# Eight batches one by one, or four pairs of batches as nine full row tiles with a written engine order

## The chip, the cores and the metric

The kernel runs on one core of one Trainium2 chip. The metric is the device time of one execution in microseconds (us): the median of several runs. Beside the runs stands one profiled execution, with the times of every instruction and DMA packet. TensorE (PE) multiplies matrices into PSUM, VectorE (DVE) and ScalarE (ACT) do element-wise work and empty PSUM, GpSimd (POOL) issues the weights' DMAs, and SyncE (SP) issues the other DMAs.

## The reference, cut to what matters

Linear attention with elu+1 as its feature map, for 8 batches, 8 heads, 576 rows and 64 columns a head, and then a mixer block on the heads put side by side (512 columns): token mixing over the 576 rows, channel mixing over the 512 columns.

```python
def phi(x):                                    # q, k, v: (8, 8, 576, 64), f32
    return np.where(x > 0, x, np.exp(x) - 1.0) + 1.0
q_p, k_p = phi(q), phi(k)
kv  = np.einsum('bhsd,bhse->bhde', k_p, v)
z   = np.sum(k_p, axis=2)
num = np.einsum('bhsd,bhde->bhse', q_p, kv)
den = np.einsum('bhsd,bhd->bhs', q_p, z)[..., None] + 1e-06
x = (num / den).transpose(0, 2, 1, 3).reshape(8, 576, 512)
h = np.maximum(x.transpose(0, 2, 1) @ w_tok1, 0.0) @ w_tok2      # 576x256, 256x576
u = x + h.transpose(0, 2, 1)
out = u + np.maximum(u @ w_ch1, 0.0) @ w_ch2                     # 512x1536, 1536x512
```

## The kernel before

One batch is 576 rows: four row tiles of 128 and one of 64, which takes as many instructions as a full one. Matmul operands are bf16, sums f32 in PSUM.

For each batch `emit_load` (L87) issues 15 DMAs on SP: q, k and v, each by row tile. A partition holds one row of the sequence; for each head 64 floats lie together in memory, so the packets are of 256 bytes. Two buffers of each are there. The weights are cast to bf16 by DMAs of POOL at the start (L58 to L73).

`emit_phi_v` (L113) makes phi on ScalarE and VectorE: exp to bf16 (L103), min with 1 (L106), then max(x, 0) plus that (L108); v is cast (L118, L120) with a column of ones behind each head, so that the product with k gives z too. `emit_kv` (L149) multiplies k and v for two heads at a time over five row tiles into one PSUM tile, which ScalarE copies into a block-diagonal `kv_sb` (L165, L167). `emit_qt` (L128) transposes q on TensorE, 20 transposes a batch, and ScalarE copies them. `emit_num_stile` (L171) gives numerator and denominator of one row tile in four matmuls into `nd_ps` (two PSUM buffers, shared with the k-v product and q's transposes under the tag "attn"); VectorE takes the reciprocal (L181) and multiplies (L182) into `x_sb`.

`emit_mm1` and `emit_mm2` are the token mixing: 10 matmuls of 512 columns, relu on ScalarE (L208), 10 more, the sum u on VectorE (L228), 20 transposes of u (L235) and their copies to `uT` (L245). `emit_mm3` (L253) is the first channel product: two halves of 288 rows, for each 12 blocks of 128 channels, 4 matmuls of 288 columns into `c_ps` (two PSUM buffers), relu on ScalarE to `cr` (L267). `emit_mm4` (L271) is the second: for each of the five row tiles 12 matmuls of 512 columns into `h2_ps` (called h_ps in the profile, L278), the sum on VectorE (L283), and the store (L285).

The last loop takes the batches in turn; attention of the next batch is written between the two channel products and, one numerator tile for each row tile, inside the second one. The order on each engine is then the scheduler's, which moves ready work forward: in the trace transposes of the next batch stand among the first channel product's matmuls.

## Time and profile before

| | us |
|---|---|
| median of 3 runs (382.64 to 384.41) | 384.29 |
| span of the profiled execution, first to last instruction | 382.6 |
| TensorE busy in it | 315.2 |
| ScalarE, VectorE busy | 168.7, 162.6 |
| first channel matmul of batch 0 starts at | 63.97 |
| one late batch, first channel product to the next one's (272.7 to 311.7) | 39.0 |

The time of the profiled execution outside its span is not shown. The page gives engines' busy time, but a matmul's time there holds its latency, so in a row of matmuls what counts is the time of the row divided by their number. Waiting is read from the idle time in brackets before an instruction, with the instruction that ended it.

### The profile page before, as it was taken

To read this page: it belongs to the slowest core of one execution; us is meant where nothing else is said; L and a number is where in the kernel's file an instruction comes from. 1 tells how busy PE (TensorE), PEld (TensorE's weight loads), DVE (VectorE), ACT (ScalarE), POOL (GpSimd) and SP (SyncE) were. 2 spreads that over 40 slices of the span, in tenths; PEclk is the share of its full clock that TensorE was granted. 3 is DMA by queue.
4 is the path that set the end of the run, shared out by engine and by line. 5 is a ranking of instruction groups with operands and counts; after the bars stand their busy time and mean duration, and the time that the engine had idled before them with its cause. 6 is when DMAs were issued, how large, how long until landed. Compare 5 with 4: busy or idle time off the path is not lost.

```text
span 382.6 us, 5083 instructions
## 1 busy us (share of the span) xinstructions
PE 315.2 (82%) x2022; PEld 178.7 (47%) x2048; DVE 162.6 (42%) x272; ACT 168.7 (44%) x297; POOL 13.0 (3%) x29
## 2 busy tenths in 40 slices
PE   0020756999879998999899988999999989978995
PEld 0020413665546545655465445645664556433642
DVE  1034467059576466456592349034402350232012
ACT  0304342780576436860884078504660366013620
POOL 7330000000000000000000000000000000000000
PEclk9999975999969999999999999999999999995999
DMA  9999999305997379637991760021002100210012
GB/s 178 205 205 207 215 214 210 70 3 158 195 207 116 77 198 212 131 84 192 203 215 32 199 139 0 2 87 38 0 2 83 43 1 2 82 41 2 0 55 71
DMA packets 121032, 41.82 MB, mean 109 GB/s; under 512 B 113520, under 2 KB 115888, under 8 KB 121008
## 3 DMA queue, kind: packets, MB, share of 16 engines
q1 hardware_dynamic: 117760, 37.76, 47.2%
q0 software_dynamic: 3248, 3.74, 5.6%
q8 instruction: 16, 0.26, 0.3%
q14 instruction: 8, 0.07, 0.1%
HBM read 35.78 MB, written 9.44 MB: 118 GB/s over the span
## 4 chain that ended last, share of the span: by engine, by line
PE 67%; SPq 11%; ACT 9%; DVE 6%; DMA 4%; issue 3%; DVEq 0%; ACTq 0%
PE c_ps L261 28%; PE h_ps L278 26%; SPq L94 11%; PE a_ps L204 4%; ACT uT L245 3%; DMA k_raw<-in_k_dram 3%; PE ut_ps L235 2%; PE kv_ps L155 2%; ACT qT L145 2%; PE h_ps L224 2%; DVE u_sb L228 2%; DVE q_p_e L108 1%; PE nd_ps L175 1%; ACT k_p_e L103 1%; ACT q_p_e L103 1%
## 5 line engine op out<-in xcount | busy, mean ns | idle before, releaser
L261 PE MATMUL c_ps<-uT,w_ch_sb 128*128 128x288 bf16 x768 | 113.3, 289 | 2.7 <-ACT uT L245 0.8
L278 PE MATMUL h_ps<-w_ch_sb,cr 128*128 128x512 bf16 (+1 forms) x467 | 105.0, 380 | 0.6
L261 PEld LDWEIGHTS <-w_ch_sb 128*128 128x128 bf16 x768 | 74.7, 98 | 38.9 <-issue 20.2
L267 ACT ACTIVATE cr<-c_ps 128x288 bf16<-128x288 f32 x192 | 77.8, 410 | 29.9 <-PE c_ps L261 23.4
L283 DVE TENSOR_TENSOR o_sb<-h_ps,u_sb 128x512 f32<-128x512 f32 (+1 forms) x40 | 27.5, 688 | 120.2 <-PE h_ps L278 116.9
L278 PEld LDWEIGHTS <-cr 128*128 128x128 bf16 (+1 forms) x480 | 47.2, 100 | 52.9 <-issue 2.1
L208 ACT ACTIVATE ar<-a_ps 128x512 bf16<-128x512 f32 x16 | 8.9, 595 | 92.0 <-PE a_ps L204 92.0
L228 DVE TENSOR_TENSOR u_sb<-h_ps,x_sb 128x512 bf16<-128x512 f32 (+1 forms) x40 | 27.5, 688 | 40.5 <-PE h_ps L224 40.5
L138 PE MATMUL qt_ps<-identity,q_p_e 128*128 128x128 bf16 x160 | 13.0, 231 | 24.2 <-POOL identity masks.py:199 24.2
L245 ACT COPY uT<-ut_ps 128x1024 bf16<-128x1024 bf16 (+1 forms) x24 | 20.9, 870 | 25.8 <-PE ut_ps L235 25.8
L235 PE MATMUL ut_ps<-identity,u_sb 128*128 128x128 bf16 x160 | 18.1, 245 | 15.5 <-DVE u_sb L228 15.3
L224 PE MATMUL h_ps<-ar,w_tok_sb 128*128 128x512 bf16 (+1 forms) x74 | 28.1, 442 | 1.7 <-ACT ar L208 1.0
L155 PE MATMUL kv_ps<-v_sb,k_p_e 128*128 128x130 bf16 (+1 forms) x160 | 18.9, 233 | 12.0 <-DVE v_sb L118 12.0
L103 ACT ACTIVATE k_p_e<-k_raw 128x2048 bf16<-128x2048 f32 (+1 forms) x16 | 20.0, 1267 | 19.7 <-DMA k_raw<-in_k_dram 14.4
L182 DVE TENSOR_TENSOR x_sb<-nd_ps,rden 128x512 bf16<-128x512 f32 (+1 forms) x40 | 26.9, 678 | 0.6
L235 PEld LDWEIGHTS <-u_sb 128*128 128x128 bf16 x160 | 10.8, 106 | 28.2 <-DVE u_sb L228 27.8
L108 DVE SCALAR_TENSOR_TENSOR q_p_e<-q_raw,q_p_e 128x2048 bf16<-128x2048 f32 (+1 forms) x16 | 23.6, 1482 | 0.2
L108 DVE SCALAR_TENSOR_TENSOR k_p_e<-k_raw,k_p_e 128x2048 bf16<-128x2048 f32 (+1 forms) x16 | 23.4, 1478 | 0.1
L138 PEld LDWEIGHTS <-q_p_e 128*128 128x128 bf16 x160 | 10.8, 104 | 26.4 <-DVE q_p_e L108 21.6
L175 PE MATMUL nd_ps<-kv_sb,qT 128*128 128x130 bf16 (+1 forms) x160 | 17.9, 242 | 6.1 <-ACT qT L145 2.8
L103 ACT ACTIVATE q_p_e<-q_raw 128x2048 bf16<-128x2048 f32 (+1 forms) x16 | 20.1, 1267 | 6.0 <-DMA q_raw<-in_q_dram 6.0
L155 PEld LDWEIGHTS <-k_p_e 128*128 128x128 bf16 (+1 forms) x160 | 12.2, 100 | 21.1 <-DVE v_sb L118 12.3
(27 smaller groups left out, 129.9 us busy)
## 6 DMA issues: line engine op xcount, KB each, us to landing
q_raw<-in_q_dram SPq DMA_DIRECT2D x32, 256.0 KB, 5.0
k_raw<-in_k_dram SPq DMA_DIRECT2D x32, 256.0 KB, 5.2
v_raw<-in_v_dram SPq DMA_DIRECT2D x32, 256.0 KB, 4.6
out_dram<-o_sb SPq DMA_DIRECT2D x32, 256.0 KB, 2.1
w_ch_sb<-in_moe_w_ch_dram POOLq DMA_DIRECT2D x4, 384.0 KB, 9.7
w_ch_sb<-in_moe_w_ch_dram POOLq DMA_DIRECT2D x12, 128.0 KB, 8.3
q_raw<-in_q_dram SPq DMA_DIRECT2D x8, 128.0 KB, 4.7
...
```

Of the source, the lines that this page charges most:

```text
L94: nc.sync.dma_start(out=tl[:sz, i, :, :], in_=src)
L103: nc.scalar.activation(out=e[:p, lo:hi], in_=flat_in[:p, lo:hi], func=AF.Exp)
L108: nc.vector.scalar_tensor_tensor(out=e[:p, lo:hi], in0=flat_in[:p, lo:hi], scalar=0.0, in1=e[:p, lo:hi], op0=ALU.max, op1=ALU.add)
L155: nc.tensor.matmul(out=kv_ps[:, j // 2, j % 2, 0:2 * (D + 1)], lhsT=k_p[:sz, i, 2 * j:2 * j + 2, :], rhs=v_sb[:sz, i, 2 * j:2 * j + 2, :], ...
L224: nc.tensor.matmul(out=h_ps[:sz], lhsT=w_tok2_sb[:, kt, 128 * ms:128 * ms + sz], rhs=ar[:, kt, :], start=(kt == 0), stop=(kt == NT - 1))
L228: nc.vector.tensor_tensor(out=u_sb[:sz, ms, :], in0=h_ps[:sz], in1=x_sb[:sz, ms, :], op=ALU.add)
L235: nc.tensor.transpose(out=ut_ps[:, nt, :], in_=u_sb[:, ms, 128 * j:128 * (j + 1)], identity=identity)
L245: nc.scalar.copy(out=dst, in_=ut_ps[:, 0:nt, :].rearrange("p (a b) c -> p a b c", b=NDM))
L261: nc.tensor.matmul(out=c_ps, lhsT=w_ch1_sb[:, kj, 128 * mc:128 * (mc + 1)], rhs=uT[:, kj, :, :].rearrange("p a b -> p (a b)")[:, SH * half ...
L267: nc.scalar.activation(out=cr[:, mc, SH * half:SH * (half + 1)], in_=c_ps, func=AF.Relu)
L278: nc.tensor.matmul(out=h2_ps[:sz], lhsT=cr[:, kc, 128 * ms:128 * ms + sz], rhs=w_ch2_sb[:, kc, :], start=(kc == 0), stop=(kc == NCH - 1))
L283: nc.vector.tensor_tensor(out=o_sb[:sz], in0=h2_ps[:sz], in1=u_sb[:sz, ms, :], op=ALU.add)
```

## The change

The kernel function is written anew. Two batches make a pair. Of each, rows 0 to 511 are four full tiles in which partition p holds the rows 4p to 4p+3, so that one head's part of a partition is 1 KB in memory; the last 64 rows of both batches make a ninth tile, one batch in each half of its partitions. It is used with operands that are zero in the other half (`vst`, `qTt`, `w1t`, `w2t`). Channel mixing of a pair runs over 1152 rows: 512 (`slot_a`) and 512 + 128 (`slot_b`) columns in the first product, nine row tiles in the second (`slot_4`). phi is max(min(exp x, 1), x + 1). The denominators get their 1e-6. PSUM has three buffers for the channel products, three for most other tiles and one for `nd_ps`.

All engines issue in the written order (`manual_schedule`). Batch 0, then batch 1, go up to their first channel product one after the other. After that each pair's channel mixing is a row of slots, 24 of the first product in turn `slot_a`, `slot_b`, then 27 of the second, four matmuls each; a plan says after which slot each step of the next pair stands. For pair 0 only the last 27 slots are left for that. The loads of a pair's chunk are issued when the phi steps before it have used the buffer. At the start chains of waits order the transfers: the weights wait for q's first chunk, the second batch's loads for the third block of the first channel weight, the second channel weight for v's first chunk of that batch, and the second pair's loads for a block of that weight.

The diff's added lines, cut ("..." marks what is left out); the removed ones are the functions above.

```diff
+    def load_chunk(nm, p, b, g):
+        hs = slice(4 * g, 4 * g + 4)
+        s = src[nm][2 * p + b, hs, 0:SM, :].rearrange("h (p r) d -> p h (r d)", r=R)
+        return nc.sync.dma_start(out=raw[nm, b][:, hs].rearrange("p h r d -> p h (r d)"), in_=s)
+
+    def load_tail(nm, p):
+        for b in range(2):
+            s = src[nm][2 * p + b, :, SM:S, :].transpose([1, 0, 2])
+            ins = nc.sync.dma_start(out=raw[nm, "t"][half[b]], in_=s)
+        return ins
+
+    def phi_flat(src_flat, dst, n):
+        e = work.tile([128, 1024], BF16, name="e", tag="e")[:, :n]
+        y = work.tile([128, 1024], BF16, name="y", tag="y")[:, :n]
+        nc.scalar.activation(out=e, in_=src_flat, func=AF.Exp)
+        nc.vector.tensor_scalar(out=y, in0=src_flat, scalar1=1.0, scalar2=None, op0=ALU.add)
+        nc.vector.tensor_scalar(out=e, in0=e, scalar1=1.0, scalar2=None, op0=ALU.min)
+        dst(e, y)
+    def phi(nm, b, g):
+        dstt = (kp if nm == "k" else qp)[b]
+        f = raw[nm, b][:, 4 * g:4 * g + 4].rearrange("p h r d -> p (h r d)")
+        def put(e, y):
+            nc.vector.tensor_tensor(
+                out=dstt[:, :, 4 * g:4 * g + 4, :].transpose([0, 2, 1, 3]),
+                in0=e.rearrange("p (h r d) -> p h r d", h=4, r=R),
+                in1=y.rearrange("p (h r d) -> p h r d", h=4, r=R), op=ALU.max)
+        phi_flat(f, put, 1024)
+    ...
+    def kv(b, g):
+        ps = ps_sm.tile([128, 2, 256], FP32, name="kv_ps", tag="sm")
+        for jj in range(2):
+            j = 2 * g + jj
+            for r in range(R):
+                nc.tensor.matmul(out=ps[:, jj, 0:2 * D1], lhsT=kp[b][:, r, 2 * j:2 * j + 2, :],
+                                 rhs=vs[b][:, r, 2 * j:2 * j + 2, :], start=(r == 0), stop=False)
+            nc.tensor.matmul(out=ps[:, jj, 0:2 * D1], lhsT=kpt[:, 2 * j:2 * j + 2, :],
+                             rhs=vst[b][:, 2 * j:2 * j + 2, :], start=False, stop=True)
+        for i in range(2):
+            nc.scalar.copy(out=kvbd[b][half[i], 2 * g:2 * g + 2, i * D1:(i + 1) * D1],
+                           in_=ps[half[i], :, i * D1:(i + 1) * D1])
+    ...
+    def nd(b, r):
+        tail = r == R
+        ps = ps_nd.tile([128, 2, 2, 256], FP32, name="nd_ps", tag="nd")
+        for j in range(HP):
+            nc.tensor.matmul(out=ps[:, j // 2, j % 2, 0:2 * D1],
+                             lhsT=qTt[b][:, j, :] if tail else qT[b][:, j, r, :],
+                             rhs=kvbd[b][:, j, :], start=True, stop=True)
+        ...
+        nc.vector.tensor_scalar(out=den, in0=v_[:, :, :, D:D1].rearrange("p j h o -> p j (h o)"),
+                                scalar1=EPS, scalar2=None, op0=ALU.add)
+        nc.vector.reciprocal(out=den, in_=den)
+        dst = xt[ps_] if tail else x[b][:, r, :]
+        nc.vector.tensor_tensor(
+            out=dst.rearrange("p (j h d) -> p j h d", j=HP, h=2), in0=v_[:, :, :, 0:D],
+            in1=den[:, :, :, None].to_broadcast([n, HP, 2, D]), op=ALU.mult)
+    ...
+    def mm3_group(mc, c0, n, on_act=True):
+        ps = ps_big.tile([128, 512], FP32, name="c_ps", tag="big")[:, :n]
+        for kj in range(NDM):
+            nc.tensor.matmul(out=ps, lhsT=wc1[:, kj, 128 * mc:128 * mc + 128],
+                             rhs=uT[:, kj, c0:c0 + n], start=(kj == 0), stop=(kj == NDM - 1))
+        dst = cr[:, mc, c0:c0 + n]
+        if on_act:
+            nc.scalar.activation(out=dst, in_=ps, func=AF.Relu)
+        else:
+            nc.vector.tensor_scalar(out=dst, in0=ps, scalar1=0.0, scalar2=None, op0=ALU.max)
+    ...
+    def slot_b(mc):
+        mm3_group(mc, 512, 512)
+        mm3_group(mc, 1024, 128, on_act=False)
+    ...
+    for nm, g in (("k", 0), ("v", 0), ("k", 1), ("v", 1)):
+        landed[nm, g] = load_chunk(nm, 0, 0, g)
+    load_tail("k", 0)
+    load_tail("v", 0)
+    landed["q", 0] = load_chunk("q", 0, 0, 0)
+    load_chunk("q", 0, 0, 1)
+    load_tail("q", 0)
+    ...
+    after(nc.gpsimd.dma_start(out=w1, in_=moe_w_tok1[0:SM, :].rearrange("(p r) t -> p r t", r=R)),
+          landed["q", 0])
+    ...
+    gate = wc1_in[NB - 2]
+    for nm in "kv":
+        for g in range(2):
+            landed[nm, 1, g] = after(load_chunk(nm, 0, 1, g), gate)
+            gate = None
+    for g in range(2):
+        load_chunk("q", 0, 1, g)
+    gate = landed["v", 1, 0]
+    ...
+    for mc in range(NCH):
+        slot_a(mc)
+    for g in range(2):
+        next_k(1, g)
+    kv(1, 0)
+    kv(1, 1)
+    for g in range(2):
+        phi("q", 1, g)
+    ...
+    qtr(1, 0)
+    qtr(1, 1)
+    for r in range(R + 1):
+        nd(1, r)
+    for mt in range(NT):
+        mm1(1, mt)
+    for r in range(R + 1):
+        mm2(0, 1, r)
+        if r in (2, 4):
+            utr(0, 4 + r - 2, 2)
+    utr(0, 8, 1)
+    for mc in range(NCH):
+        slot_b(mc)
+    ...
+    chunks = [(0, 0), (0, 1), (1, 0), (1, 1), ("t", 0)]
+    def do_k(p):
+        def one(b, g):
+            next_k(b, g)
+            if p + 1 < NP:
+                for nm in "kv":
+                    load_tail(nm, p + 1) if b == "t" else load_chunk(nm, p + 1, b, g)
+    ...
+            first = p == 0
+            if first:
+                ks = [24, 25, 27, 28, 30]
+                for s, fn in zip(ks, do_k(1)):
+                    at(s, fn, -1)
+                qs = [31, 32, 33, 34, 34]
+                pos = {"kv": [32, 32, 33, 33], "qt": [35, 36, 38, 39, 37],
+                       "nd": [38, 39, 40, 40, 41, 41, 42, 42, 43, 43],
+                       "m1": [43, 44, 45, 46],
+                       "m2": [46, 46, 47, 47, 47, 48, 48, 49, 49, 50],
+                       "ut": [48, 49, 50, 50, 50]}
+            else:
+                qs = [0, 1, 2, 3, 4]
+                pos = {"kv": [0, 1, 2, 3], "qt": [4, 5, 7, 8, 6],
+                       "nd": [9, 10, 11, 12, 13, 14, 15, 16, 17, 18],
+                       "m1": [17, 19, 21, 22],
+                       "m2": [24, 25, 26, 27, 28, 29, 30, 31, 32, 33],
+                       "ut": [28, 30, 35, 37, 38]}
+    ...
+            if p + 2 < NP:
+                ks = [44, 45, 47, 48, 50] if not first else [50, 50, 50, 50, 50]
+                for s, fn in zip(ks, do_k(p + 2)):
+                    at(s, fn, 9)
```

Here `kv` is the product of k and v, `qt` q's transposes, `nd` a numerator tile, `m1` and `m2` the token mixing, `ut` the transposes of u; `do_k` makes phi of k, casts v and issues the next loads of both, `do_q` the same for q. A numerator tile's VectorE steps are an addition of 1e-6, the reciprocal and the multiplication.

## Rows read from the trace of the kernel before

L12 is line 12 of the kernel before. The table by stretches has: stretch, its us, busy us (x instructions) of PE, of its weight loads, of DVE, ACT and POOL, the granted TensorE clock (1.00 is 2.4 GHz), the share of time in which the 16 DMA engines were busy, GB/s. A timeline row has: start us, us, engine, line, operation, out<-in, shape, x count, and in brackets the idle time before and what ended it. A group by shape has: line, engine, operation, shapes, x count, then busy us and mean ns of one, then idle us before and what ended it. A queue's row in the DMA view has: packets, MB, share of 16 engines; MB of a weight are those written, in bf16.

**Rows 1.** The page, part 1: busy time (share of the span) xinstructions.

```profile
PE 315.2 (82%) x2022; PEld 178.7 (47%) x2048; DVE 162.6 (42%) x272; ACT 168.7 (44%) x297; POOL 13.0 (3%) x29
```

**Rows 2.** Table by stretches, four of them; columns as told above.

```profile
50.00:60.00 10.00, 5.14 (x20) 1.77 (x19) 6.89 (x9) 4.11 (x5) 0.00 (x0) 0.62 1.35 214
...
299.00:311.70 12.70, 11.20 (x101) 6.83 (x102) 6.97 (x16) 7.08 (x11) 0.00 (x0) 1.00 0.05 12
...
311.70:338.00 26.30, 26.12 (x152) 14.85 (x154) 4.13 (x7) 9.31 (x23) 0.00 (x0) 1.00 0.11 41
...
338.00:351.00 13.00, 9.08 (x36) 2.97 (x35) 4.66 (x9) 3.11 (x4) 0.00 (x0) 0.67 0.05 11
```

**Rows 3.** The chain in order of time: start us, us, what.

```profile
63.97 0.64 PE c_ps L261 x2
...
319.77 1.14 PE c_ps L261 x8
...
324.41 13.01 PE h_ps L278 x59
...
338.04 1.79 PE a_ps L204 x7
...
350.39 0.64 PE c_ps L261 x2
```

**Rows 4.** Timeline of TensorE and ScalarE in channel mixing and attention.

```profile
73.83 0.65 PE L261 MATMUL c_ps<-uT,w_ch_sb 128*128 128x288 bf16 x4
...
74.31 2.03 PE L155 MATMUL kv_ps<-v_sb,k_p_e 128*128 128x130 bf16 x20
...
304.32 0.78 PE L138 MATMUL qt_ps<-identity,q_p_e 128*128 128x128 bf16 x11
...
319.31 0.90 ACT L267 ACTIVATE cr<-c_ps 128x288 bf16<-128x288 f32 x2 [0.25 <-PE c_ps L261]
```

**Rows 5.** Groups by shape, ScalarE and VectorE.

```profile
L103 ACT ACTIVATE k_p_e<-k_raw 128x2048 bf16<-128x2048 f32 x8 | 15.3, 1912 | 18.0 <-DMA k_raw<-in_k_dram 12.7 <-DVE q_p_e L108 5.3
...
L106 DVE TENSOR_SCALAR k_p_e<-k_p_e 128x2048 bf16<-128x2048 bf16 x8 | 5.4, 678 | 11.5 <-ACT k_p_e L103 11.5
...
L106 DVE TENSOR_SCALAR k_p_e<-k_p_e 64x512 bf16<-64x512 bf16 x8 | 2.2, 277 | 0.0
...
L108 DVE SCALAR_TENSOR_TENSOR k_p_e<-k_raw,k_p_e 128x2048 bf16<-128x2048 f32 x8 | 18.2, 2280 | 0.0
...
L118 DVE CAST v_sb<-v_raw 128x2048 bf16<-128x2048 f32 x8 | 9.7, 1211 | 0.0
...
L182 DVE TENSOR_TENSOR x_sb<-nd_ps,rden 128x512 bf16<-128x512 f32 x32 | 21.6, 679 | 0.4
...
L165 ACT CAST kv_sb<-kv_ps 64x260 bf16<-64x260 f32 x8 | 3.0, 377 | 12.3 <-PE kv_ps L155 12.3
```

**Rows 6.** Timeline of VectorE and TensorE around single numerator tiles.

```profile
58.73 2.88 DVE L108 SCALAR_TENSOR_TENSOR k_p_e<-k_raw,k_p_e 128x2048 bf16<-128x2048 f32 x2
...
308.64 0.64 DVE L182 TENSOR_TENSOR x_sb<-nd_ps,rden 128x512 bf16<-128x512 f32 x1
...
309.38 0.41 PE L175 MATMUL nd_ps<-kv_sb,qT 128*128 128x130 bf16 x4
...
311.19 0.40 PE L175 MATMUL nd_ps<-kv_sb,qT 128*128 128x130 bf16 x4
...
311.63 0.21 DVE L181 RECIPROCAL rden<-nd_ps 128x8 f32<-128x8 f32 x1
```

**Rows 7.** DMA view of 249:338, 46:60 and 14:21 us, in this order.

```profile
q1 hardware_dynamic: 1888, 3.41, 10.8%
...
DMA packets 11875, 2.99 MB, mean 213 GB/s; under 512 B 11875, under 2 KB 11875, under 8 KB 11875
...
q0 software_dynamic: 832, 1.19, 92.8%
```

**Rows 8.** Timeline of VectorE, the last instruction on an engine.

```profile
378.74 0.68 DVE L283 TENSOR_TENSOR o_sb<-h_ps,u_sb 64x512 f32<-64x512 f32 x1 [2.02 <-PE h_ps L278]
```

More of the change, by code (lines that the diff above doesn't have):

```diff
@@ L36 @@
     DCH = moe_w_ch1.shape[1]
-    NS = (S + 127) // 128
-    s_sizes = [min(128, S - 128 * i) for i in range(NS)]
+    R = 4
+    SM = 128 * R
+    ST = S - SM
     NT = DTOK // 128
@@ L290 @@
[L290 to L317 removed]
+    work = ctx.enter_context(tc.tile_pool(name="work", bufs=2))
@@ new lines, with after @@
+    xt = const("xt", [128, DM])
+    ar = [const(f"ar{b}", [128, NT, DM]) for b in range(2)]
+    u = [const(f"u{i}", [128, 9, DM]) for i in range(2)]
+    uT = const("uT", [128, NDM, 9 * 128])
+    cr = const("cr", [128, NCH, 9 * 128])
+    half = [slice(0, 64), slice(64, 128)]
+    ctx.enter_context(tc.manual_schedule())
+    src = {"q": q, "k": k, "v": v}
+    sync_dep = mybir.DependencyInfo(mybir.DependencyClass.Sync, mybir.DependencyReason.DATA)
+    def after(ins, other):
+        if other is not None:
+            tc.add_manual_dep(ins.ins, other.ins.name, sync_dep, reason="order of transfers")
+        return ins
@@ new lines, in phi, with phi_tail, put @@
+    def phi(nm, b, g):
[7 more added lines that the diff above has]
+        phi_flat(f, put, 1024)
+    def phi_tail(nm):
+        dstt = kpt if nm == "k" else qpt
+        def put(e, y):
+            nc.vector.tensor_tensor(out=dstt.rearrange("p h d -> p (h d)"), in0=e, in1=y,
+                                    op=ALU.max)
+        phi_flat(raw[nm, "t"].rearrange("p h d -> p (h d)"), put, 512)
@@ new lines, in vcast, with vcast_tail @@
+    def vcast(b, g):
+        nc.vector.tensor_copy(out=vs[b][:, :, 4 * g:4 * g + 4, 0:D].transpose([0, 2, 1, 3]),
+                              in_=raw["v", b][:, 4 * g:4 * g + 4])
+    def vcast_tail():
+        for b in range(2):
+            nc.vector.tensor_copy(out=vst[b][half[b], :, 0:D], in_=raw["v", "t"][half[b]])
+    def kv(b, g):
[10 more added lines that the diff above has]
+                           in_=ps[half[i], :, i * D1:(i + 1) * D1])
@@ new lines, in mm1, with mm2 @@
+    def mm1(b, mt):
+        ps = ps_sm.tile([128, DM], FP32, name="a_ps", tag="sm")
+        ms = slice(128 * mt, 128 * mt + 128)
+        for r in range(R):
+            nc.tensor.matmul(out=ps, lhsT=w1[:, r, ms], rhs=x[b][:, r, :],
+                             start=(r == 0), stop=False)
+        nc.tensor.matmul(out=ps, lhsT=w1t[:, b, ms], rhs=xt, start=False, stop=True)
+        nc.scalar.activation(out=ar[b][:, mt, :], in_=ps, func=AF.Relu)
+    def mm2(p, b, r):
+        tail = r == R
+        ps = ps_sm.tile([128, DM], FP32, name="h_ps", tag="sm")
+        for kt in range(NT):
+            nc.tensor.matmul(out=ps, lhsT=w2t[:, kt, b, :] if tail else w2[:, kt, r, :],
+                             rhs=ar[b][:, kt, :], start=(kt == 0), stop=(kt == NT - 1))
+        if tail:
+            h = half[b]
+            nc.vector.tensor_tensor(out=u[p % 2][h, 8, :], in0=ps[h], in1=xt[h], op=ALU.add)
+        else:
+            nc.vector.tensor_tensor(out=u[p % 2][:, 4 * b + r, :], in0=ps, in1=x[b][:, r, :],
+                                    op=ALU.add)
@@ new lines, in slot_a, with slot_4 @@
+    def slot_a(mc):
+        mm3_group(mc, 0, 512)
+    def slot_b(mc):
+        mm3_group(mc, 512, 512)
+        mm3_group(mc, 1024, 128, on_act=False)
+    held = {}
+    def slot_4(p, t, part):
+        if part == 0:
+            held["h2"] = ps_big.tile([128, DM], FP32, name="h2_ps", tag="big")
+        ps = held["h2"]
+        for kc in range(4 * part, 4 * part + 4):
+            nc.tensor.matmul(out=ps, lhsT=cr[:, kc, 128 * t:128 * t + 128], rhs=wc2[:, kc, :],
+                             start=(kc == 0), stop=(kc == NCH - 1))
+        if part < 2:
+            return
+        o = outp.tile([128, DM], FP32, name="o_sb", tag="o_sb")
+        nc.vector.tensor_tensor(out=o, in0=ps, in1=u[p % 2][:, t, :], op=ALU.add)
+        if t < 8:
+            b, r = divmod(t, 4)
+            nc.sync.dma_start(
+                out=out[2 * p + b, 0:SM, :].rearrange("(p r) d -> r p d", r=R)[r], in_=o)
+        else:
+            for b in range(2):
+                nc.sync.dma_start(out=out[2 * p + b, SM:S, :], in_=o[half[b]])
```

438 lines of the change are left out of this document (188 added, 250 removed).

## The prediction

> **What bounds the kernel now.** I read the page's first part, then a table by stretches, the chain in order of time, the timeline of single stretches, and the groups by shape for prices. TensorE is busy 82% of the span, no other engine over 47% [rows 1]. The table shows why the rest is missing [rows 2]. A late batch takes 39.0 us: 26.3 us of channel mixing (311.7 to 338) with TensorE busy without a break, and 12.7 us of attention and token mixing before it (299 to 311.7), where it is busy 11.2. Early stretches are worse: from 50 to 60 TensorE is busy for half the time and is granted 0.62 of its clock (a mix of 1.2 and 2.4 GHz), and the last batch, with no next batch to mix in, takes 13 us at 0.67 for the same step. Inside channel mixing the two products differ. The second runs 59 matmuls of 512 columns in 13.01 us, 0.217 each with latency [rows 3]. The first takes 1.14 us for 8 of 288 columns, 0.143 each, although four alone take 0.65 with some 0.17 of latency, 0.12 each [rows 3, 4]. ScalarE in turn idles 0.25 us before each pair of evictions [rows 4]: two PSUM buffers let neither engine get ahead. So the bound is TensorE in channel mixing and, at the start and between batches, chains of short steps over three engines.
>
> **What falls away.** Columns first. Per pair of batches, first product: 12 x 2 x 2 x 4 matmuls of 288 columns at 0.143, 27.5 us, become 96 of 512 at 0.217 and 48 of 128. The trace has no accumulating matmul of 128 columns; the rows on both sides are transposes (11 in 0.78, less 0.17: 0.056) and the k-v product of 130 columns (20 in 2.03: 0.09) [rows 4]. I take 0.09, the accumulating one: 20.9 + 4.3 = 25.2 us. At 0.056 it is 1.6 less a pair. Second product: 120 matmuls become 108, 26.0 to 23.4 us. Small products and transposes per pair: k-v 40 x 0.09, transposes 72 and numerators 40 x 0.057, token mixing 40 x 0.217, together 18.7. So a pair needs 67.2 us of TensorE, against 78 now: 10.8 saved, 43 in all if nothing else moved.
>
> **What comes in its place.** Every engine now issues in written order, so I add up the stages by what stands in front of what.
>
> Prices for 1024 elements: VectorE's fixed part is 0.143 (277 ns at 512, 678 at 2048) [rows 5]. A cast from f32 is 0.68 (1211 at 2048), and so the new x+1; min is 0.41; exp 1.05 (1912 at 2048, ScalarE). The new max of two bf16 tensors has no row. From above it is bounded by the two-tensor step with an f32 input, 2280 at 2048, hence 1.21, from below by min, 0.41. Cast against min shows the price fall to 0.56 when the f32 input becomes bf16; the same share of 1.21 is 0.68, which I take. (The Trainium skill, "VectorE: DVE Perf Modes", The perf-mode tier table, has bf16 tensor_tensor at twice the f32 rate; no run here shows it.) Neighbours that don't depend on each other overlap by some 0.08: the two steps of line 108, 2.28 and 0.68, take 2.88 [rows 6]. A k chunk with its v cast is then 2.2 us, a q chunk 1.6, all k work of a pair 10.4, all q work 7.35.
>
> The numerator tile has one PSUM buffer now. One turn: 0.44 from its first matmul to the reciprocal, 0.2 for the added epsilon, 0.1 to 0.2 for the reciprocal, 0.68, hand-overs of 0.03 to 0.1 (line 182 ends at 309.28, the next matmul starts at 309.38): 1.63 us, 1.85 at 1.2 GHz [rows 5, 6] (an estimate from 0.057 more for each of its four matmuls).
>
> Loads: 2 KB stores moved 3.41 MB in 10.8% of 89 us, 355 GB/s; 256-byte loads saturate at 213 [rows 7]. By packet that is 92 and 19 ns; linearly between, 1 KB takes 50 ns, 324 GB/s (bounds 213 and 355). The first k and v with tails land at about 11 us, q with its tail at 15.4. Weights wait for q's first chunk (POOL has the other weights queued behind); at 1.19 MB written in 92.8% of 7 us [rows 7] the first channel weights are in by 30, needed at 43. The second half's loads wait on SP for these, land near 45, and are needed at 54; the second weights land near 50, needed at 104. These gates cost nothing while that cover holds.
>
> - Stage 1, to the first channel matmul: k and v ready at 12.4 (tails landed at 11, their last steps 1.4), k-v product about 3.1 at a slow clock, its copies 0.8 (2 x 0.38 [rows 5]; they stand before q's exp on ScalarE), q 4.7 (exps 1.05 + 1.05 + 0.6, then the last chunk's and the tail's min and max), reordering of the second token weight 2.0 on VectorE before the numerators; then 4 turns of 1.85, and token mixing with transposes as in the last batch, 338.04 to 350.39, 12.35 [rows 3]. Sum 42.8.
> - Stage 2, first product of batch 0: 48 x 0.217 + 1 for the slow start: 11.4.
> - Stage 3, batch 1 up to its first channel matmul. Nothing stands between: its exps queue behind the twelve evictions on ScalarE, and everything follows. To the numerators 14.2 (last eviction 0.8, exp 1.05, first k chunk's min, max and v cast 1.8, second chunk 2.2, its k-v product 1.3, copies 0.8, two q exps 2.1, min and max 1.1, transposes 1.0, copies 1.05, and hand-overs inside 1.0), numerators 8.0, token mixing 12.35: 34.6.
> - Stage 4, first product of batch 1: 12 x 1.23 + 0.6 = 15.3.
> - Stage 5, second product of pair 0 with all of pair 1's attention in 27 slots, 23.4 us of matmuls. VectorE binds: 10.4 + 7.35, nine output additions 5.8, ten numerator turns 16.3, ten token additions 6.4, and about 10 where it waits for TensorE (before the first numerator, and during the first token product): 56.2, + 3 at 1.2 GHz after the wait before the k-v product: 59.
> - Stage 6: pair 2's k work stands whole behind slot 50 on VectorE, and the k-v product of slot 0 needs its tail, last of all: 10.4 + 0.9 = 11.3.
> - Stage 7, pair 1: 67.2 less the 1.8 already done, + 3.5 because numerator turns (1.63) are longer than their slots (1.28), + 1.5 because ScalarE has exps, copies and evictions in slots 0 to 8: 70. Then pair 3's k work begins only at slot 44: 12.3 us of VectorE against 6.1 of matmuls, wait and k-v product 7.2, + 1 of slow clock: 8.2.
> - Pair 2: 70. Pair 3, with nothing mixed in: 25.2 + 23.4 = 48.6. End: addition and store, 3.9 (378.74 to 382.6 now) [rows 8].
>
> Sum: 42.8 + 11.4 + 34.6 + 15.3 + 59 + 11.3 + 70 + 8.2 + 70 + 48.6 + 3.9 = 375.1 us of span. The profiled span is 382.6 and the median 384.3; what lies around the span isn't shown, so I add that 1.7: **377 us**. The 43 us saved on columns are nearly eaten by stages 3, 5 and 6.
>
> The clock, at 0.62 to 0.67 where TensorE waits often [rows 2], is in the sum as 5.6 us of slow restarts besides the slower steps of stages 1 and 3. The Trainium skill ("TensorE: Matmul & The Clock Gate", Loop structure matters more than you think) warns that idle gaps between bursts put the array back to its slow clock, which speaks against stages 3, 5 and 6; without any such restart the sum would be 371, with them 377.
>
> **Rivals.**
> A. Max of two bf16 tensors costs 1.21, not 0.68. It decides wherever VectorE binds: 0.53 for each of some 24 chunks, tails half: 4 chunks in stage 3 and about as many in stage 1 (partly behind exp), 8 in stage 5, 4 in stage 6, 4 at slot 44, about 13 us: 390, slower. For it: the only two-tensor rows from SBUF are at that price. Against: their input is f32. It turns the sign from about 0.9 on.
> B. The clock stays at 1.2 GHz through stage 5. Its 42 us of TensorE work take 83, 24 more than 59: 401. Against: after the last batch's sparse stretch the first product is back at 1.14 per eight within a few us.
> C. The clock is high in stages 1 and 3: 40 token matmuls at 0.217 less each, numerator turns at 1.63, transposes at half: 14 us less; with no slow restarts either, 358. Against: 0.67 in the same step of the last batch.
> D. 1 KB packets are no better than 213 GB/s: stage 1 starts some 5 us later, and batch 1's data become late by a few: 384, no change.
> E. The written order doesn't hold up as I read it, and VectorE's steps slip into each other's gaps, stages 5 and 6 near TensorE's own 42 and 1: about 351. Against: each engine's queue is strictly the written one.
>
> **How the numbers follow.** Forecast 0.50, A 0.17, B 0.06, C 0.14, D 0.08, E 0.05. About 0.5% can be told from no change: 382.4 to 386.2. The forecast itself, with its terms' bounds (1 KB rate, 128 columns at 0.056, reciprocal), spreads from 367 to 388: 0.36 faster, 0.08 same, 0.06 slower. With C, E and a little of D: faster 0.57; same 0.08 + 0.05 of D = 0.13; slower 0.06 + A + B + 0.01 = 0.30. The range leaves out B, E and the outer halves of the rest: 358 to 394.
>
> **What would show it.** First channel matmul at about 43 us and not 64 [rows 3]; TensorE nearly idle from 54 to 89; channel mixing at 0.217 per 512 columns with no wait on evictions; in the last 49 us no idle time of TensorE; VectorE without a gap before slot 0 of pair 1 and TensorE waiting some 10 us there for the k-v product's inputs; about 7 us again one pair later. The max row near 0.68, else A. I am wrong most easily in stage 5, where five queues are followed by hand, and in the clock.

## The result, and the profile after

The changed kernel takes **360.9 us** (359.3 to 361.7) against 383.5 for the kernel before in the same session: a ratio of 0.941, interval 0.937 to 0.945. So it is 5.9% faster, where the forecast was 377 us, 1.9%. The sign and the range (358 to 394) held; the size did not.

The first two parts of the page after (engines' busy time, then 40 slices of 8.9 us):

```profile
span 357.5 us, 4635 instructions
PE 280.5 (78%) x1776; PEld 148.2 (41%) x1776; DVE 185.4 (52%) x406; ACT 147.2 (41%) x229; POOL 10.0 (3%) x19
PE   0256864389949659808989999939889999999995
DVE  6574325442599663698575362787571642211221
PEclk9999995589987999977999999989999999999999
```

Against [rows 1] TensorE's work falls from 315 to 280.5 us, 34.7 less, but its idle time grows from 67 to 77. The page shows where (slices counted from 1): 6 to 9 (stage 3), 12 to 15 (stage 5), 18 (stage 6) and 27 (the hand-over from pair 1 to pair 2).

Now the chain that ended last (start, us, what), cut to the joints of the stages and two rows of stage 5:

```profile
30.39 1.71 PE a_ps L207 x4
32.52 0.99 PE a_ps L207 x4
...
39.38 10.53 PE c_ps L239 x48
...
71.33 1.71 PE a_ps L207 x4
73.46 1.00 PE a_ps L207 x4
...
80.33 12.99 PE c_ps L239 x92
...
107.94 1.71 PE h_ps L261 x4
...
113.73 0.86 PE h_ps L261 x4
...
306.58 23.50 PE c_ps L239 x144
330.08 23.32 PE h_ps L261 x108
353.43 0.69 DVE o_sb L266
```

The first channel matmul stands at 39.38 and no longer at 63.97 [rows 3]; batch 1 needs from 49.9 to 80.33 before its first product; pair 3, with nothing mixed in, runs 252 matmuls without a break in 46.8 us. The waits between pairs are in TensorE's timeline (start, us, line, operation, count, idle time before it and what ended it):

```profile
106.05 0.27 PE L155 MATMUL kv_ps<-vst,kpt 128*128 128x130 bf16 x1 [4.53 <-DVE vst L146]
162.46 0.27 PE L155 MATMUL kv_ps<-vst,kpt 128*128 128x130 bf16 x1 [7.72 <-DVE vst L146]
166.90 0.39 PE L153 MATMUL kv_ps<-vs,kp 128*128 128x130 bf16 x4
238.13 0.27 PE L155 MATMUL kv_ps<-vst,kpt 128*128 128x130 bf16 x1 [6.10 <-DVE vst L146]
```

All three waits are for the last step of a pair's k work on VectorE, the places that the forecast named. Starts of the first group of each product in the same timeline give a table by stage (us). Beside the changed kernel stand the runs that change one thing of it, one profiled execution each:

| kernel | 1 | 2 | 3 | 4 | 5 | pair 1, first product, with 6 | second | pair 2, first product, with the hand-over | second | pair 3 | end |
|---|---|---|---|---|---|---|---|---|---|---|---|
| forecast | 42.8 | 11.4 | 34.6 | 15.3 | 59 | 51.6 | 29.7 | 48.5 | 29.7 | 48.6 | 3.9 |
| changed | 39.4 | 10.5 | 30.4 | 13.0 | 56.5 | 51.2 | 29.6 | 46.0 | 29.6 | 47.0 | 4.1 |
| e1_tile_by_tile | 42.4 | 10.5 | 36.3 | 14.6 | 55.7 | 52.4 | 29.6 | 46.4 | 29.6 | 46.9 | 4.1 |
| e2_double_128 | 40.7 | 10.5 | 31.3 | 15.7 | 55.5 | 53.8 | 29.6 | 47.1 | 29.6 | 49.6 | 4.1 |
| e3_k2_in_gaps | 40.5 | 10.5 | 31.3 | 13.0 | 67.7 | 39.6 | 29.6 | 46.5 | 29.6 | 47.0 | 4.0 |
| e4_k3_early | 40.1 | 10.5 | 30.4 | 13.0 | 56.5 | 51.2 | 29.6 | 39.2 | 29.6 | 47.0 | 4.1 |
| e6_two_nd | 38.0 | 10.5 | 27.9 | 20.5 | 53.8 | 51.9 | 30.5 | 45.8 | 29.6 | 55.4 | 4.1 |
| e9_spread | 40.7 | 12.6 | 17.9 | 14.9 | 45.7 | 37.6 | 31.8 | 39.2 | 29.6 | 46.9 | 4.1 |

(In the forecast's row a pair's second product is the measured one, and its first the rest of the forecast's sum.) A second profile of the changed kernel, taken beside the last run, has a span of 360.8 us with 41.2 in stage 1 and 31.3 in stage 3 (in stage 1 all ten matmuls of the first token product stand 0.43 us apart in it, in the first profile only about the first half), so differences below about 2 us in these two stages are not read.

### The profile page after: what moved, and what is told of

It is laid out like the page before. It is cut to its first block, busy times and chain, and to the rows that moved or that the text cites. A ratio compares the mean times of both kernels' runs of the same rounds, so it can differ in the third digit from the quotient of the medians.

```text
span 357.5 us, 4635 instructions
## 1 busy us (share of the span) xinstructions
PE 280.5 (78%) x1776; PEld 148.2 (41%) x1776; DVE 185.4 (52%) x406; ACT 147.2 (41%) x229; POOL 10.0 (3%) x19
## 4 chain that ended last, share of the span: by engine, by line
PE 64%; DVE 23%; ACT 6%; issue 3%; DMA 2%; SPq 1%; ACTq 0%
PE h_ps L261 22%; PE c_ps L239 21%; DVE x L198 6%; PE nd_ps L186 5%; PE a_ps L207 4%; PE h_ps L216 4%; DVE y L117 3%; PE kv_ps L153 3%; DVE vs L141 2%; DMA k_rawt<-in_k_dram 2%; DVE e L118 2%; PE tp L229 2%; DVE kp L126 2%; DVE den L196 2%; ACT e L116 2%
## 5 line engine op out<-in xcount | busy, mean ns | idle before, releaser
L239 PE MATMUL c_ps<-uT,wc 128*128 128x512 bf16 (+1 forms) x576 | 103.8, 330 | 1.7 <-ACT uT L233 1.6
L261 PE MATMUL h_ps<-wc,cr 128*128 128x512 bf16 x432 | 101.8, 381 | 0.0
L243 ACT ACTIVATE cr<-c_ps 128x512 bf16<-128x512 f32 x96 | 57.8, 604 | 49.7 <-PE c_ps L239 49.5
L239 PEld LDWEIGHTS <-wc 128*128 128x128 bf16 x576 | 49.9, 99 | 45.8 <-issue 4.6
L261 PEld LDWEIGHTS <-cr 128*128 128x128 bf16 x432 | 41.3, 98 | 45.7 <-issue 1.2
L266 DVE TENSOR_TENSOR o_sb<-h_ps,u 128x512 f32<-128x512 f32 x36 | 24.8, 690 | 41.7 <-PE h_ps L261 41.7
L233 ACT COPY uT<-tp 128x1024 bf16<-128x1024 bf16 (+1 forms) x20 | 18.2, 928 | 42.1 <-PE tp L229 42.0
L222 DVE TENSOR_TENSOR u<-h_ps,x 128x512 bf16<-128x512 f32 x32 | 21.3, 686 | 20.0 <-PE h_ps L216 19.9
L186 PE MATMUL nd_ps<-kvbd,qT 128*128 128x130 bf16 x128 | 15.1, 244 | 17.0 <-DVE x L198 13.0
L198 DVE TENSOR_TENSOR x<-nd_ps,den 128x512 bf16<-128x512 f32 x32 | 22.1, 691 | 1.1
L207 PE MATMUL a_ps<-x,w 128*128 128x512 bf16 x64 | 18.5, 416 | 0.0
```

The costliest lines, as they stand in the source:

```text
L186: nc.tensor.matmul(out=ps[:, j // 2, j % 2, 0:2 * D1], lhsT=qTt[b][:, j, :] if tail else qT[b][:, j, r, :], rhs=kvbd[b][:, j, :], start=Tr ...
L198: nc.vector.tensor_tensor(out=dst.rearrange("p (j h d) -> p j h d", j=HP, h=2), in0=v_[:, :, :, 0:D], in1=den[:, :, :, None].to_broadcast( ...
L207: nc.tensor.matmul(out=ps, lhsT=w1[:, r, ms], rhs=x[b][:, r, :], start=(r == 0), stop=False)
L222: nc.vector.tensor_tensor(out=u[p % 2][:, 4 * b + r, :], in0=ps, in1=x[b][:, r, :], op=ALU.add)
L239: nc.tensor.matmul(out=ps, lhsT=wc1[:, kj, 128 * mc:128 * mc + 128], rhs=uT[:, kj, c0:c0 + n], start=(kj == 0), stop=(kj == NDM - 1))
L243: nc.scalar.activation(out=dst, in_=ps, func=AF.Relu)
```

## The experiments

All were timed in three rounds against the kernel before on the same chip; "+x us" is the difference of the two ratios times 384. With the intervals of both ratios, such a difference is uncertain by some 2 us (by 2.9 for the first run). **Theory:** the stages are the right ones and VectorE's written order sets them, while three terms were too dear: the token step in stages 1 and 3, the 128-column matmuls, and the restarts of the clock. **Rivals** stand in the expectations.

**The token step, in the changed kernel.** Each tile is reordered right behind its own product:

```diff
-        if r in (2, 4):
-            utr(0, r - 2, 2)
+        if r < 4:
+            utr(0, r, 1)
```

(in the second batch `utr(0, 4 + r, 1)` for every r).

> In the two token-mixing steps that nothing hides (stages 1 and 3) each row tile is reordered right behind its own token product, as the kernel before does, instead of two tiles after three or two products. Theory: the forecast mis-sized these steps because it took 12.35 us from a step with this tile-by-tile order; each turn makes TensorE wait for the token addition (0.69 us and hand-overs), three turns more in each step, so about 2.5 us more in each: 365 to 367 us. Rival: the order is not what made the old step long (its clock alone did): 361 to 362.

Ratio 0.958 (0.952 to 0.964), 6.6 us more, somewhat over the theory. Its chain, the two ends of the step in stage 1 and then two turns in stage 3:

```profile
30.64 1.71 PE a_ps L207 x4
...
42.42 10.53 PE c_ps L239 x48
...
82.72 0.87 PE h_ps L216 x2
83.61 0.70 DVE u L222
84.36 0.61 PE tp L229 x4
84.97 0.87 PE h_ps L216 x2
85.86 0.70 DVE u L222
```

Every tile now pays product, addition and reordering in a row: 2.25 us in these rows of stage 3, with TensorE at its lower level (granted 0.50 from 82.1 to 89.4; 0.43 for each 512 columns), and 1.61 in stage 1, where the last products run at the full level. From first token product to first channel product the step takes 11.8 us in stage 1 and 15.1 in stage 3 (74.38 to 89.46), against 9.0 in both stages of the changed kernel. The second profile of the changed kernel, with a slow start like this one, has 9.9 in stage 1, so the order by itself costs 2 to 3 us, and in stage 3 the clock adds at least as much. The executions differ in the same way: one was granted 0.939 of the clock over its span and took 365.6 us, the other three 0.926 and 369.1 to 370.6. The 12.35 us of the forecast belong to this order, not to the one in the diff.

**The same order, the other way round, in the kernel before.** There the transposes of line 235 move behind all five products:

```diff
+        for ms in range(NS):
             for j in range(NDM):
                 if nt == 0:
```

> The kernel before with one edit: the five token products of a batch run first and all reordering of u follows, instead of tile by tile. Theory: the 12.35 us of the last batch's token step, which the forecast took for stages 1 and 3, was long because of this order; that step falls by about 3 us in the last batch and in the first, and by less in the batches between, where TensorE has other work: 373 to 379. Rival: the order doesn't matter in this kernel (two PSUM buffers hold the products back anyway): 383 to 385.

Ratio 0.956 (0.954 to 0.958), 17 us less, more than any step of mine foresaw. The chain of its last batch:

```profile
325.23 2.17 PE a_ps L204 x9
327.47 1.09 ACT ar L208 x2
329.02 0.70 DVE u_sb L228
...
332.44 1.94 ACT uT L246 x2
334.41 0.67 PE c_ps L262 x4
```

9.2 us from first token product to first channel product, where [rows 3] has 12.35. The granted clock of that step is 1.00 here and 0.68 there, so the 3.2 us are the order's and the clock's together. The first channel product of batch 0 starts at 59.34 instead of 63.97, and most batches between gain too. TensorE's transposes of u among the groups by shape (count, busy time, mean ns, idle time before them and what ended it), the kernel before and then this one:

```profile
L235 PE MATMUL ut_ps<-identity,u_sb 128*128 128x128 bf16 x160 | 18.1, 245 | 15.5 <-DVE u_sb L228 15.3
```
```profile
L236 PE MATMUL ut_ps<-identity,u_sb 128*128 128x128 bf16 x160 | 13.0, 220 | 5.1 <-ACT uT L246 4.8 <-DVE u_sb L228 0.2
```

The 15.3 us of waiting for VectorE's additions before the transposes are gone. They are not the whole account: over the kernel TensorE's idle time falls by 9 us (67.4 to 58.0) and its busy time by 8 (315.2 to 307.2), with 0.99 of the clock granted instead of 0.96 to 0.97.

**The price of a 128-column matmul.**

```diff
-        for kj in range(NDM):
+        for _ in range(1 if on_act else 2):
+          for kj in range(NDM):
```

> Each of the 48 groups of four 128-column matmuls in the first channel product is computed twice into the same PSUM tile (result unchanged), 192 matmuls more. Theory: such a matmul costs 0.056 us on the path, as the records of the changed kernel say: 10.7 us more, 371 to 372. Rival: 0.09, as the forecast took: 17.3 us more, 378.

Ratio 0.9606 (0.959 to 0.962), 7.6 us more for 192 matmuls, 0.040 each. Stage 4 grows by 2.7, pair 1's first product by 2.6 and pair 3 by 2.6, 0.054 to 0.056 each; pair 2's by 1.1 only, where other waits take part of it up. So 0.09 was wrong; in these rows an accumulating matmul costs what a transpose does. The k-v product agrees: ten of 130 columns between 166.90 and 167.47 in the timeline above, 0.057 each. The 0.09 of [rows 4] is another thing. In the old k-v product every fifth matmul has 64 rows, and in the same trace, at full clock, such matmuls stand out (TensorE's timeline before):

```profile
98.03 0.39 PE L155 MATMUL kv_ps<-v_sb,k_p_e 128*128 128x130 bf16 x4
98.80 0.87 PE L155 MATMUL kv_ps<-v_sb,k_p_e 64*128 64x130 bf16 x7
```

Four of 128 rows take 0.39 with the 0.22 that a single one takes, so they stand 0.057 apart; in the second row two of the seven have 64 rows, and they stand 0.11 apart on average. Why the 64-row matmuls cost more is not shown. The changed kernel has none: its tail has 128 rows, half of them zeros.

**The ring of two PSUM buffers, in the kernel before.** Halves of 288 columns in four buffers:

```diff
-                c_ps = ps_c.tile([128, SH], FP32, name="c_ps", tag="c")
+                if mc % 2 == 0:
+                    c_ps = ps_c.tile([128, SH], FP32, name="c_ps", tag="c")
+                else:
+                    c_ps = ps_small.tile([128, DM], FP32, name="c_ps", tag="ps_small")[:, :SH]
```

> The kernel before with one edit: the groups of 288 columns in the first channel product take turns in four PSUM buffers (two of them idle there otherwise) instead of two. Theory: the 0.143 us for 288 columns against 0.12 for four alone is the ring of two buffers; with four, eight matmuls take 0.96 to 1.0 us in place of 1.14, over 12 x 8 such groups 14 to 17 us: 367 to 371. Rival: the ring doesn't bind, the matmuls themselves are that long: 382 to 385; then only the number of columns carries the gain of the wide groups.

Ratio 0.963 (0.960 to 0.966), 14 us less, as the theory had it. Its chain shows 93 such matmuls in one piece, 0.122 each, against 0.143 [rows 3]:

```profile
301.76 11.39 PE c_ps L264 x93
```

The forecast gave the first product's wider tiles 2.3 us in each pair, 9 in all (16 with a 128-column matmul at 0.055). The ring alone is worth 14.

**Wide columns without the third buffer, in the kernel before.**

```diff
-        for half in range(2):
-            for mc in range(NCH):
-                c_ps = ps_c.tile([128, SH], FP32, name="c_ps", tag="c")
+        for mc in range(NCH):
+            for c0, n in ((0, 512), (512, S - 512)):
+                c_ps = ps_c.tile([128, 512], FP32, name="c_ps", tag="c")[:, :n]
```

> The kernel before with one edit: its first channel product runs over 512 and 64 columns in turn instead of 288 and 288. Theory: what bounds 288 columns is the ring of two PSUM buffers, and a 512-column group (0.87) covers its own eviction (0.60); 12 x (0.87 + 0.2) us in place of 13.7 in each batch, 0.9 to 1.4 us each, 7 to 11 in all: 373 to 377. Rival: the narrow group's eviction now makes the next wait in the same ring, and nothing is gained: 383 or more.

Ratio 1.049 (1.046 to 1.053): 19 us slower. It is the rival's wait, and dearer than the rival had it. Two lines of ScalarE's timeline, and one of TensorE's between them:

```profile
343.37 0.71 ACT L267 ACTIVATE cr<-c_ps 128x512 bf16<-128x512 f32 x2 [1.00 <-PE c_ps L261]
345.07 0.71 ACT L267 ACTIVATE cr<-c_ps 128x512 bf16<-128x512 f32 x2 [1.00 <-PE c_ps L261]
```
```profile
344.99 0.59 PE L278 MATMUL h_ps<-w_ch_sb,cr 128*128 128x512 bf16 x2
```

With two buffers every wide group goes into the same one, so a turn is group, latency and eviction in a row: 1.70 us, against 1.14 for two halves. Matmuls of the second product slip into these waits (line 278), so the loss is 19 us and not 12 x 0.56 x 8 = 54.

**Two numerator tiles, in the changed kernel.** `ps_big` and `ps_sm` have two buffers instead of three, `ps_nd` two instead of one.

> The numerator tile gets two PSUM buffers, and the channel products and the small tiles two instead of three. Theory: a numerator turn falls from 1.63 (1.84 at the slow clock) to VectorE's own 1.06; over 10 turns in stage 5 and 4 in each of stages 1 and 3 that is about 5.5 + 3 + 3 us, less what smaller rings cost: 350 to 354. Rival: the small ring takes it back (the third buffer hid the evictions and the token additions): 361 or more.

Ratio 0.958 (0.955 to 0.962), 6.6 us more: the rival. In the table both effects stand side by side: stages 1, 3 and 5 are shorter by 1.4, 2.5 and 2.7 (less than the theory's sum), stage 4 and pair 3 longer by 7.5 and 8.4. The reason is that of the run before, a turn of 1.71 us (start to start, stage 4):

```profile
79.82 1.25 PE L239 MATMUL c_ps<-uT,wc 128*128 128x512 bf16 x8 [0.46 <-ACT cr L243]
80.88 0.60 ACT L243 ACTIVATE cr<-c_ps 128x512 bf16<-128x512 f32 x1 [1.11 <-PE c_ps L239]
81.53 1.25 PE L239 MATMUL c_ps<-uT,wc 128*128 128x512 bf16 x8 [0.46 <-ACT cr L243]
```

So where nothing stands between the groups of the first product (stage 4, pair 3), the pairing pays only together with the third buffer. In pairs 1 and 2, which have other work between them, two buffers change that product by 0.7 and -0.2 us.

**Pair 2's k work inside stage 5.** `ks` for pair 0 becomes `[36, 37, 44, 45, 46]` instead of five times 50.

> Pair 2's k work, 10 us of VectorE, which stands whole behind slot 50 of pair 0, is written behind slots 36, 37, 44, 45 and 46. Theory: VectorE has gaps of some 10 us in stage 5 (before the first numerator and during the first token product), so most of the 7.7 us that TensorE waits in stage 6 goes: 353 to 356. Rival: VectorE is full in stage 5, so the work only moves and stage 5 grows by what stage 6 loses: 360 to 362.

Ratio 0.936 (0.933 to 0.938), 2 us less, which the intervals don't tell from none: the rival. Stage 5 grows by 11.1 us, and what follows shrinks by 11.7. Two windows, the changed kernel's stages 5 and 6 and this kernel's stage 5 (stretch, length, busy time of PE, PEld, DVE, ACT and POOL with counts, granted clock, DMA share, GB/s):

```profile
93.30:149.90 56.60, 45.03 (x305) 24.75 (x302) 41.72 (x87) 21.97 (x32) 0.00 (x0) 0.94 0.54 164
149.90:163.10 13.20, 2.06 (x18) 1.26 (x16) 10.77 (x22) 7.83 (x10) 0.00 (x0) 0.71 0.67 210
```
```profile
95.43:163.09 67.66, 52.10 (x304) 27.75 (x302) 52.21 (x108) 25.96 (x37) 0.00 (x0) 0.80 0.69 207
```

VectorE did 10 us more there in 11 us more. Its gaps are half a microsecond in each numerator turn, shorter than most of a chunk's steps (0.43 to 0.70), and TensorE is granted less of its clock (0.80 for 0.94). These gaps took up nothing of the chain.

**Pair 3's k work earlier.** `ks` for pair 1 becomes `[34, 36, 38, 40, 42]`.

> Pair 3's k work is written behind slots 34, 36, 38, 40 and 42 of pair 1 instead of 44, 45, 47, 48 and 50. Theory: the wait before the k-v product at the hand-over is 12.3 us of VectorE against 6.1 us of matmuls; begun 10 slots earlier it is done in time, and the 6.1 us of idle TensorE go: 354 to 355. Rival: something else (the data of pair 3, a buffer) sets that wait: 361.

Ratio 0.920 (0.918 to 0.922), 8 us less; the stage with the hand-over falls from 46.0 to 39.2. The theory holds: only the place in VectorE's order made this wait.

**VectorE's load.** One line under `if keep_min[0]:`, false from pair 1 on.

> The minimum of phi is left out for pairs 1 to 3 (the function computed is then another). It takes 0.43 us of VectorE for each of 1024 elements. Theory: VectorE sets the time in stage 5 (10 chunks, 4.0 us), in stage 6 (2.0) and at the hand-over from pair 1 to pair 2 (2.0), so about 8 us less: 352 to 354. Rival: these stages wait for a chain through TensorE and ScalarE, and VectorE's own time is not it: 358 to 361.

Ratio 0.924 (0.921 to 0.927), 6.5 us less for 10.6 us less of VectorE's work (174.8 of 185.4). Between the two. Where the edit was to act, its profile has half of the 8 us expected: 2.0 in stage 5, 1.3 in the first product of pair 1 with stage 6, 0.7 in that of pair 2 with the hand-over. So VectorE's own time counts there, but about half of what it is relieved of turns into waits, above all for ScalarE's exps: VectorE's waits for them, before minimum and maximum, grow from 22 to 26 us.

**256-byte loads.** Rows `"h (r p) d -> r p h d"`, four transfers for each chunk, and the same order of rows in the token weights and the output.

> Row tiles are taken with 128 neighbouring rows instead of every fourth, so that q, k and v are loaded in 256-byte stretches (four transfers for each chunk) and all else stays. Theory: at 213 GB/s the first k and v land some 5 us later, and what comes after stage 1 is covered: 365 to 367. Rival: the size of the loads carries much of the gain, batch 1's and pair 1's data come late as well: 375 or more. Third: no cost at all, 361.

Ratio 0.948 (0.946 to 0.951), 2.8 us more. ScalarE's second and third exps start as their data land, the changed kernel first:

```profile
8.16 1.06 ACT L116 ACTIVATE e<-k_raw 128x1024 bf16<-128x1024 f32 x1 [2.40 <-DMA k_raw<-in_k_dram]
11.68 0.63 ACT L116 ACTIVATE e<-k_rawt 128x512 bf16<-128x512 f32 x1 [2.46 <-DMA k_rawt<-in_k_dram]
```
```profile
10.15 1.06 ACT L119 ACTIVATE e<-k_raw 128x1024 bf16<-128x1024 f32 x1 [2.39 <-DMA k_raw<-in_k_dram]
13.78 0.63 ACT L119 ACTIVATE e<-k_rawt 128x512 bf16<-128x512 f32 x1 [2.57 <-DMA k_rawt<-in_k_dram]
```

2 us at the start (from 3 to 12 us the DMA engines move 222 GB/s here and 305 in the changed kernel), no later loss clear of noise: neither the theory's 4 to 6 nor the rival's 14. The 1 KB loads are a small part of the gain. (The order of the transfers by itself was not tried.)

**The clock in stage 3.** 38 matmuls that nobody reads (8, 12, 3 and five times 3; the expectation miscounts them as 35), in TensorE's waits:

```diff
+    def idle(n):
+        ps = ps_big.tile([128, 512], FP32, name="idle_ps", tag="big")
+        for i in range(n):
+            nc.tensor.matmul(out=ps, lhsT=identity, rhs=wc1[:, 0, 0:512], start=True, stop=True)
```

> 35 matmuls of 512 columns whose result nobody reads are put into TensorE's waits in stage 3 (behind the first channel product, behind the k-v product, behind the reordering of q and behind each numerator). Theory: stage 3 has a part of its 30.4 us from the slow clock (numerator turns of 1.84 instead of 1.63, the first token products, the k-v product and reorderings at half speed); at full clock it is 2.5 to 3.5 us shorter: 358 to 359. Rival: the clock doesn't return, or these matmuls stand in the way: 361 to 364.

Ratio 0.932 (0.930 to 0.934), 3.4 us less: the theory. The whole of stage 3 is now granted the full clock, where the changed kernel has 0.66, with two slices of its page at 0.5. The two rows by stretches, the changed kernel first:

```profile
49.90:80.33 30.43, 15.04 (x97) 8.75 (x98) 15.89 (x33) 10.84 (x16) 0.00 (x0) 0.66 0.80 199
50.10:78.10 28.00, 19.17 (x135) 9.44 (x133) 15.89 (x33) 10.81 (x16) 0.00 (x0) 1.00 0.86 221
```

The Trainium skill ("TensorE: Matmul & The Clock Gate", Loop structure matters more than you think) says that a long wait between matmuls, there for a DMA, makes TensorE go cold. The trace agrees for stage 3, where the waits are for VectorE and ScalarE: 30.4 us at 0.66 of the clock, 28.0 with the waits filled.

**Another order of the same work.** The core of the edit:

```diff
-    for mc in range(NCH):
-        slot_a(mc)
-    for g in range(2):
-        next_k(1, g)
+    next_k(1, 0)
+    slot_a(0)
+    slot_a(1)
+    next_k(1, 1)
...
-                qs = [31, 32, 33, 34, 34]
-                pos = {"kv": [32, 32, 33, 33], "qt": [35, 36, 38, 39, 37],
-                       "nd": [38, 39, 40, 40, 41, 41, 42, 42, 43, 43],
+                qs = [24, 25, 29, 31, 26]
+                pos = {"kv": [25, 25, 26, 26], "qt": [27, 28, 32, 33, 29],
+                       "nd": [30, 31, 32, 33, 34, 36, 37, 38, 39, 40],
...
+        if mc in (2, 5, 8):
+            k1[mc // 3 + 1]()
```

> Nothing is left out. The same work in another written order: batch 1's attention between the first channel products of batch 0 (its data have landed by 39 us); pair 1's k work in stages 3 and 4; its numerators of the first batch ahead of the second batch's q work; three chunks of pair 2's k work late in stage 5 and two in pair 1's first slots, with pair 2's attention some four slots later; pair 3's k work from slot 36 of pair 1 on. Theory: VectorE's order, not TensorE, sets stages 3, 5, 6 and the hand-over: stage 3 falls by about 11 us, 5 and 6 together from 68 to 48, the hand-over by 6, while pair 1 and stage 4 grow by 2 to 3: 324 to 332. Rival: what is moved only pushes other waits, as with pair 2's k work alone: 345 to 355.

**323.1 us**, ratio 0.840 (0.838 to 0.841), the fastest here, just under the theory's range. Two windows, stages 3 and 5 (columns as above):

```profile
53.30:71.20 17.90, 10.60 (x61) 4.94 (x60) 10.91 (x24) 5.58 (x8) 0.00 (x0) 0.81 1.15 296
86.00:131.70 45.70, 41.80 (x304) 22.90 (x302) 36.10 (x78) 20.42 (x31) 0.00 (x0) 1.00 0.53 160
```

Stage 5 is now TensorE's own 42 and little else, since its k work lies in stages 3 and 4 and the first batch's token products run while VectorE does the second batch's q. TensorE idles 47 us in all, 77 in the changed kernel. Which of the moves carries how much was not taken apart, save for pair 3's k work (e4_k3_early).

**Is the gain that of pairing?** Both edits of b2_transposes_last and b3_four_buffers on the kernel before, with the changed kernel beside it:

> The kernel before with both edits of the two runs above on it: four PSUM buffers in the first channel product, and the reordering of u behind all token products. Theory: the two losses lie in different stages, so the gains add, 17 + 14 us: 352 to 356, less time than the pairing of batches as it was written takes. Rival: they overlap (the shorter token step starves the next batch's attention, which then waits behind the channel product): 360 to 366.

> The changed kernel itself, beside the run above on the same chip, so that the two are compared there: 360 to 362, as measured with the change.

**351.3 us**, ratio 0.913 (0.910 to 0.917), and 361.8, ratio 0.940 (0.937 to 0.944). The two edits add up (33.7 us, for 17 and 14), and single batches with them are 10.5 us faster than the pairs as written. From its page:

```profile
PE 294.1 (84%) x2048; PEld 179.1 (51%) x2048; DVE 162.2 (46%) x272; ACT 162.9 (47%) x297; POOL 13.1 (4%) x29
```

Its TensorE has 13.6 us more to do than the pairs, and 21 us less idle time (56 of 350.0 against 77 of 357.5). So the gain of the change isn't shown to be that of pairing. Nor is the contrary: a written order without pairs wasn't tried, and how much of the 323 us of e9_spread rests on the pairs stays open.

## Why the prediction was right in kind and wrong in size

Measured less forecast, by the table (sum -17.6 us of span). Two terms of the sum failed, the first in its mechanism, the second in its size:

- **The token step in stages 1 and 3, priced at 12.35 us each: -6.7.** The 12.35 us of [rows 3] belong to an order in which each tile is added and reordered before the next product counts, at 0.68 of the clock. The diff showed that `utr` stands behind three and behind five products, and the step takes 9.0 us in both stages (30.39 to 39.38, 71.33 to 80.33). e1_tile_by_tile brings the old price back in stage 1 (11.8), b2_transposes_last takes it from the kernel before. A row was carried over with its structure unread.
- **128 columns at 0.09 instead of 0.055: 1.7 us in stage 4 and in each of the three pairs, -6.7; the k-v product another 1.3 in each of pairs 1 and 2, -2.6. Together the largest miss.** I had both bounds and chose the upper one because its row accumulates. e2_double_128 decides for the lower, and the row's 0.09 comes with its 64-row matmuls.
- **Restarts of the clock: the sum nearly right, the places not.** Stages 2 and 4 start at full speed (12 groups at 0.877, 12 slots at 1.083), -1.6. After the waits of 4.53, 7.72 and 6.10 us for VectorE, TensorE does come back at its lower level (granted 0.52 from 106.05 to 111.40, 0.50 from 162.46 to 165.70 and from 238.13 to 239.60): in stage 5 the four matmuls at 107.94 take 1.71 us, those at 113.73 0.86. By the spacing of the matmuls (0.107 for 0.057, 0.427 for 0.216) I estimate 2.5 us in stage 5, where the forecast has 3, 1.3 at the hand-over for 1, and 1.6 in stage 6, where it has none. That the total of 5.4 is close to the forecast's 5.6 is luck. In stage 3 the clock cost 2.4 to 3.4 us (e8_warm), and this lay in steps already taken slow.
- **Stage 6: +2.2.** Chunks start 2.27 us apart, the first exp stands behind the last token addition and a copy of u, and the unpriced restart is in it.
- **Not traced term by term:** the rest, some 2 us less, most of it in stage 5 (56.5 for 59).
- **What held:** the chunk prices (cast 0.691, minimum 0.429, exp 1.06), the numerator turn (1.63, and 1.84 in stages 1 and 3), 0.217 for each 512 columns, the hand-over's wait (6.10 for 6.2), the end (4.1 for 3.9), and that VectorE's order sets stage 6 and the hand-over and in part stage 5 (e4_k3_early, e5_no_min, e9_spread).

Four rows of VectorE after, two for prices and two starts of one numerator turn (groups by shape; then its timeline):

```profile
L126 DVE TENSOR_TENSOR kp<-e,y 128x1024 bf16<-128x1024 bf16 x16 | 11.1, 692 | 0.5
L141 DVE CAST vs<-v_raw 128x1024 bf16<-128x1024 f32 x16 | 11.1, 691 | 0.0
```
```profile
119.34 0.17 DVE L194 TENSOR_SCALAR den<-nd_ps 128x8 f32<-128x8 f32 x1 [0.50 <-PE nd_ps L186]
120.97 0.17 DVE L194 TENSOR_SCALAR den<-nd_ps 128x8 f32<-128x8 f32 x1 [0.50 <-PE nd_ps L186]
```

Rival A falls with the first: the maximum of two bf16 tensors takes 0.69, not 1.21. The Trainium skill ("VectorE: DVE Perf Modes", The perf-mode tier table) has bf16 tensor_tensor at twice the f32 rate. The trace agrees: 0.69 us for 1024 elements, where half of the 1.21 without its fixed part, and that part of 0.14 again, makes 0.68. B falls: stage 5 has 0.94 of the clock. C was half right: the token step was quick, by its order and in part by its clock (granted 0.87 from 71.33 to 80.33), but the numerator turns stayed at 1.84. D falls twice: from 3 to 12 us the loads come at 305 GB/s, not 213, and e7_256B puts the price of 256 bytes at 3 us, not 5 and more. E falls: stages 5 and 6 take 56.5 and 13 us, with the wait of 7.72 where the written order puts it. That such slack can be had by another written order is shown by e9_spread (45.7 in stage 5, and 37.6 instead of 51.2 in pair 1's first product with stage 6).

One sentence failed in its meaning: that the 43 us saved on columns are nearly eaten by stages 3, 5 and 6. They are not columns. The 78 us of a pair are twice the 39.0 of a late batch, with its waits; by the forecast's own prices a pair's work was 72.6 us and falls to 67.2, some 22 us for four pairs. The 9 of them that belong to the first product can be had, and more, from the ring without pairing (14); and 17 more lay in the tile order and its clock, which the forecast didn't count among the kernel before's losses at all. (A slip beside: the terms of stage 7 add up to 70.4, not 70.)
